# Softmax-free attention, PReLU MLP and soft MoE on one core: reciprocal of the denominator spread by DMA, head pairs of Q three slots apart, K pairs sooner

## The chip, the cores and the metric

The kernel runs on one core of a Trainium2 chip (trn2). The metric is the device time in microseconds of one execution, median of several. TensorE (PE) multiplies, VectorE (DVE) and ScalarE (ACT) work elementwise, GpSimd (POOL) does the reductions over partitions, SyncE (SP) issues every DMA of this kernel, in the order in which they stand in its program.

## The reference

Three stages follow each other on 4608 tokens (8 sequences of 576) of width 512 (8 heads of 64), all in float32, w_in and w_out given as float64.

```python
def phi(x):                                            # w_phi: 64 x 128
    proj = x @ w_phi
    proj = proj - np.max(np.abs(proj), axis=-1, keepdims=True)
    return np.concatenate([np.exp(proj), np.exp(-proj)], axis=-1)
q_p, k_p = phi(q), phi(k)
kv = np.einsum('bhsf,bhsd->bhfd', k_p, v);  z = np.sum(k_p, axis=2)
num = np.einsum('bhsf,bhfd->bhsd', q_p, kv)
den = np.einsum('bhsf,bhf->bhs', q_p, z)[..., None] + 1e-06
x = num / den                                          # attention, 4608 x 512
h = x @ w_in                                           # 512 x 2048
g = np.maximum(h, 0.0) + alpha * np.minimum(h, 0.0)
x = g @ w_out                                          # 2048 x 512
logits = x @ moe2_phi                                  # 32 slots of 8 experts
slot_input = softmax(logits, over tokens).T @ x
slot_out[e] = np.maximum(slot_input[e] @ w1[e], 0.0) @ w2[e]
out = softmax(logits, over slots) @ slot_out
```

## The kernel before, in words

**Blocks and slots.** The tokens are cut into NB = 12 blocks of BT = 384. A block has NC = 16 slots, one for each 128 columns of w_in. In a slot `gemm(n, c)` (L505) issues twelve matmuls of 128x384 in the fp32r format into one PSUM bank `ph`: each of four head pairs k contributes w_hi·x_hi, w_hi·x_lo and w_lo·x_hi, where x is split into `xhi` and `xlo` and w_in likewise. `leaky` (L510 to L520) turns the bank into `gT`, and `turn_g` transposes it on VectorE (L532) and multiplies four of them at a time with `wpr` (w_out times phi, L540). The other matmuls of the kernel (K, Q, V, logits) are in plain fp32, two passes of TensorE for each instruction (the profile counts passes: a group x8 is four instructions).

**K and Q.** `k_pair` (32 of them, two heads of one sequence each) makes the features of K (L289, L280 to L284), the sums K·V (`pkv`, L333 and L339) and turns them (L355) into two tiles, `kv` and `zt`, of which KVB = 6 are kept. `q_pair` (four to a block) projects Q (`pq`, L403), takes the largest absolute value on GpSimd (L415), makes the features `qe` (L425) and calls `attend`: `num` (L435) and `den` (L442). `den` has four column groups of 32 partitions, one for each head of the pair and each half of the features; the sum over the halves isn't made there. A block of 384 may reach into two sequences, and then `segments` cuts both into two pieces.

**The division, `q_finish`.** ScalarE copies `den` and adds 1e-6 (L458); a fp32 matmul with a matrix of zeros and ones (`densum`, L460) adds the halves; VectorE takes the reciprocal of 128x384 (L464); ScalarE and VectorE split it into two fp32r halves `rhl` (L469, L470); eight matmuls with a selecting matrix (`sel`, L477 and L478, two for each head pair) spread it over the 128 partitions of `num`; VectorE multiplies (L484), ScalarE rounds to `xhi` (L485) and VectorE makes `xlo` (L486). `xhi`, `xlo` and `num` have one buffer each, so a head pair of `xhi` is written once the last matmul of the block before has read it.

**Order.** `at(slot, phase, fn)` files each piece of work under a slot and a phase, and the loop at L690 writes the program slot by slot. A list scheduler then orders each engine's instructions by the data they wait for and by their place in that program. Pairs of Q for block n stand at slots 16(n−1)−6, −2, +2 and +6 and `q_finish` at 16(n−1)+11; pair i of K (from i = 8) at slot 6i−42.

**Beside that.** In the first hundred microseconds `conv` (L183 to L214) turns w_in and w_out from float64 words into fp32, mostly on VectorE. wpr needs w_out, so g of blocks 0 and 1 is stored to DRAM (`gT_d`, L521) and read back (`reload`, L522 to L526) in ten extra steps behind slots 84 and 132 (VB = [4, 7]): four tiles at a time into two buffers of 768 KB, `vg0` and `vg1`. From slot 152 on `fetch` fills buffers that have come free with pieces of w_out, w1 and w2 for the soft MoE, in one fixed order; the last of them go into buffers of the tail.

## Time and profile before

| | us |
|---|---|
| median of 3 runs | 1057.03 (1055.14 to 1058.01) |
| profiled execution, its own time | 1057.16 |
| its span, first to last instruction | 1055.4 |
| TensorE busy | 984.1 (93%), mean granted clock 0.964 |
| VectorE busy | 773.8 (73%) |
| ScalarE busy | 469.8 (45%) |
| GpSimd busy | 149.2 (14%) |

Busy time is the time in which at least one instruction of the engine is running. Matmuls are pipelined: each is shown from its start to its modelled end, so the ends of neighbours overlap, and what a group takes on TensorE is the distance from its start to the start of the next group. The timeline gives start and duration of a group of like instructions, and in brackets how long the engine had been idle before it and what ended that.

### The profile page before, as it was taken

To read this page: it belongs to the slowest core of one execution; us is meant where nothing else is said; L and a number is where in the kernel's file an instruction comes from. 1 tells how busy PE (TensorE), PEld (TensorE's weight loads), DVE (VectorE), ACT (ScalarE), POOL (GpSimd) and SP (SyncE) were. 2 spreads that over 40 slices of the span, in tenths; PEclk is the share of its full clock that TensorE was granted. 3 is DMA by queue.
4 is the path that set the end of the run, shared out by engine and by line. 5 is a ranking of instruction groups with operands and counts; after the bars stand their busy time and mean duration, and the time that the engine had idled before them with its cause. 6 is when DMAs were issued, how large, how long until landed. Compare 5 with 4: busy or idle time off the path is not lost.

```text
span 1055.4 us, 21864 instructions
## 1 busy us (share of the span) xinstructions
PE 984.1 (93%) x9038; PEld 685.2 (65%) x9038; DVE 773.8 (73%) x1552; ACT 469.8 (45%) x908; POOL 149.2 (14%) x88
## 2 busy tenths in 40 slices
PE   3787998998999999999999999999999999998994
PEld 1445776774676776676666776767667767787353
DVE  3999989879767578587878687687888486874133
ACT  3876867776444245144235344343334343200133
POOL 2201214121111212121112111121112221000000
PEclk7898999998999999999999999999999999999995
DMA  5343653653010111010401111110401200769879
GB/s 199 120 141 125 193 188 114 225 178 100 9 31 31 39 31 38 20 51 19 163 10 38 32 39 31 31 38 19 160 19 46 96 8 2 249 226 327 261 235 309
DMA packets 71986, 110.60 MB, mean 105 GB/s; under 512 B 7248, under 2 KB 47312, under 8 KB 71888
## 3 DMA queue, kind: packets, MB, share of 16 engines
q1 hardware_dynamic: 71888, 109.22, 32.0%
q8 instruction: 71, 1.16, 0.4%
q14 instruction: 27, 0.22, 0.1%
HBM read 89.27 MB, written 19.92 MB: 103 GB/s over the span
## 4 chain that ended last, share of the span: by engine, by line
PE 71%; DVE 3%; DMA 2%; ACT 1%; issue 1%; DVEq 0%; ACTq 0%; SPq 0%
PE ph L505 34%; PE num L435 5%; PE pS L602 5%; PE pkv L333 5%; PE pl L540 4%; PE den L442 3%; PE pq L403 3%; PE pk L289 2%; DMA out_dram<-os 2%; PE pso L819 1%; PE pe L782 1%; PE sel L477 1%; PE pt L355 1%; PE pr L558 1%; PE densum L460 1%; PE pkv L339 1%
## 5 line engine op out<-in xcount | busy, mean ns | idle before, releaser
L505 PE MATMUL ph<-xhi,w 128*128 128x384 f32 x1536 | 435.2, 351 | 6.5 <-DVE gT L515 4.4
L505 PEld LDWEIGHTS ph<-xhi,w 128*128 128x128 f32 x1536 | 279.0, 189 | 76.8 <-issue 41.5
L505 PE MATMUL ph<-xlo,w 128*128 128x384 f32 x768 | 255.1, 340 | 0.0
L415 POOL PARTITION_ALL_REDUCE mb<-pj x48 | 140.4, 2928 | 553.0 <-ACT pj L409 450.1
L505 PEld LDWEIGHTS ph<-xlo,w 128*128 128x128 f32 x768 | 143.6, 188 | 12.6 <-issue 6.1
L515 DVE SCALAR_TENSOR_TENSOR gT<-gT,alpha_neg,ph 128x384 f32<-128x384 f32 x104 | 62.9, 605 | 77.3 <-ACT ph L514 76.5
L532 DVE STREAM_TRANSPOSE gb<-gT 128x384 f32<-128x384 f32 x192 | 105.6, 566 | 5.7 <-DMA gT<-gT_d 1.9
L513 ACT ACTIVATE gT<-ph 128x384 f32<-128x384 f32 x104 | 50.8, 489 | 114.8 <-PE ph L505 114.0
L425 ACT ACTIVATE qe<-pj 128x768 f32<-128x768 f32 x92 | 73.9, 839 | 59.5 <-DVE pj L419 56.2
L517 DVE TENSOR_SCALAR gT<-ph,alpha_sb 128x384 f32<-128x384 f32 x88 | 53.8, 613 | 46.2 <-PE ph L505 45.8
L333 PE MATMUL pkv<-kp,vt 128*64 128x256 f32 (+1 forms) x640 | 85.0, 400 | 1.1 <-DVE wpr L250 1.1
L435 PE MATMUL num<-qe,kv 128*64 128x192 f32 (+1 forms) x496 | 70.9, 417 | 0.0
L283 ACT ACTIVATE kp<-kp 128x512 f32<-128x512 f32 (+1 forms) x80 | 46.8, 586 | 51.6 <-DVE kp L282 51.1
L333 PEld LDWEIGHTS pkv<-kp,vt 128*64 128x64 f32 (+1 forms) x640 | 41.3, 140 | 39.4 <-issue 17.1
L280 DVE TENSOR_REDUCE mx<-pk 128x4 f32<-128x512 f32 (+1 forms) x80 | 50.2, 627 | 11.4 <-PE pk L289 9.7
L602 PE MATMUL pS<-gb,d 32*32 32x256 f32 x2304 | 55.0, 385 | 0.3 <-DVE logits L594 0.2
L403 PE MATMUL pq<-qraw,wp 64*128 64x384 f32 x192 | 48.9, 562 | 6.7 <-DMA qraw<-in_qT_dram 4.1
L446 ACT COPY num<-num 128x384 f32<-128x384 f32 x48 | 22.8, 475 | 67.1 <-PE num L435 64.2
L409 ACT COPY pj<-pq 128x768 f32<-128x768 f32 x44 | 35.2, 799 | 36.3 <-PE pq L403 36.3
L419 DVE TENSOR_TENSOR pj<-pj,mb 128x768 f32<-128x768 f32 x48 | 46.6, 971 | 6.0 <-POOL mb L415 6.0
L282 DVE TENSOR_TENSOR kp<-pk,mx 128x512 f32<-128x512 f32 (+1 forms) x80 | 50.2, 627 | 0.8 <-PE pkv L333 0.2
L514 ACT ACTIVATE ph<-ph 128x384 f32<-128x384 f32 x104 | 50.6, 487 | 0.0
(191 smaller groups left out, 1345.6 us busy)
## 6 DMA issues: line engine op xcount, KB each, us to landing
w<-in_w_dram SPq DMA_DIRECT2D x58, 256.0 KB, 5.7
qraw<-in_qT_dram SPq DMA_DIRECT2D x48, 192.0 KB, 2.4
out_dram<-os SPq DMA_DIRECT2D x18, 512.0 KB, 3.7
raw<-in_w_in_dram SPq DMA_DIRECT2D x16, 512.0 KB, 3.6
raw<-in_w_out_dram SPq DMA_DIRECT2D x16, 512.0 KB, 4.2
gT_d<-gT SPq DMA_DIRECT2D x32, 192.0 KB, 2.0
gT<-gT_d SPq DMA_DIRECT2D x8, 768.0 KB, 5.2
pf<-in_w_dram SPq DMA_DIRECT2D x21, 256.0 KB, 6.0
```

The lines of the kernel that those rows point to most:

```text
L333: return lambda: nc.tensor.matmul(pkv[64 * j:64 * j + 64, 0:256], vt[:, 64 * j:64 * j + 64], feats(t, j).rearrange("p s f -> p (s f)"), st ...
L403: lambda j=j, sl=slice(64 * j, 64 * j + 64): nc.tensor.matmul(pq[j][:, 0:BT], wp[sl], st["qraw"][sl], start=True, stop=True)
L415: nc.gpsimd.partition_all_reduce(mb, pj, 128, bass_isa.ReduceOp.absmax)
L425: nc.scalar.activation(st["e", s], pj, AF.Exp, scale=(1.0, -1.0)[s])
L435: lambda s=s, j=j: nc.tensor.matmul(num[64 * j:64 * j + 64, o:o + w], kvs[:, s, 64 * j:64 * j + 64], st["e", s][:, j, o:o + w], start=(s = ...
L505: gemm_last[0] = nc.tensor.matmul(h, (w_in_hi, w_in_lo)[a][c][:, 128 * k:128 * k + 128], (xhi, xlo)[b][:, k, :], start=(i == 0), stop=(i = ...
L513: nc.scalar.activation(gT, h, AF.Relu, scale=-1.0)
L514: nc.scalar.activation(h, h, AF.Relu)
L515: nc.vector.scalar_tensor_tensor(out=gT, in0=gT, scalar=alpha_neg[:, c:c + 1], in1=h, op0=ALU.mult, op1=ALU.add)
L517: nc.vector.tensor_scalar(out=gT, in0=h, scalar1=0.0, scalar2=alpha_sb[:, c:c + 1], op0=ALU.min, op1=ALU.mult)
L532: nc.vector.transpose(out=gb[n, c // 8][:, c % 8, :], in_=gT)
L602: lambda j=j, i=i, h=h: nc.tensor.matmul(pS[i][32 * (j % 4):32 * (j % 4) + 32, 256 * h:256 * h + 256], st["d"][32 * i:32 * i + 32, 32 * j: ...
```

## The change

- **Denominator.** `den` is now written by eight matmuls of 192 columns for each head pair, whatever the sequences: the tile holds the four column groups (head, half of the block) at 192 columns each, and the sum over feature halves and head pairs is left in PSUM. VectorE adds 1e-6 and takes the reciprocal of 128x192; two DMAs write it to DRAM (`rc_d`), and two more read it back with a step of zero over 64 partitions into `bc`, 128x1536. VectorE multiplies `num` by `bc`, all from SBUF. The matrices `densum` and `densel` with their setup, the matmuls `densum` and `sel`, and the split `rhl` are gone.
- **Places.** Pairs of Q stand three slots apart and `q_finish` at 16(n−1)+7, the read-back `widen` a slot later, division and `scale` six slots later; the division is held behind the last `leaky` or `conv` instruction of the slots up to there (`mark`). KVB is 8, and K pairs come up to eight slots sooner.
- **Read-back of g.** Two tiles at a time in three buffers `vg`, and four of the sixteen tiles through the ring of `gT`, which has five buffers.
- **Fetches.** `bc` and `vg` give three pieces each where `rhl`, `densel`, `vg0` and `vg1` gave eight; the pool `pf` opens at slot 168 in place of 170.

```diff
-KVB = 6
+KVB = 8
...
+    rc_d = [dram.tile([2, 32, 2, HB], F32, name=f"rc_d{i}") for i in range(2)]
...
-            for b, o, w in segments(n):
-                kvs, zt = kv_t[NP * b + p]
+            for s in (1, 0):
                 together([
-                    lambda g=g: nc.tensor.matmul(
-                        den[32 * g:32 * g + 32, o:o + w], zt[:, g, :], st["e", g % 2][:, g // 2, o:o + w],
-                        start=(p == 0 and o == 0), stop=(p == NP - 1 and o + w == BT))
-                    for g in (3, 1, 2, 0)])
+                    lambda j=j, h=h, zt=kv_t[NP * ((n * BT + h * HB) // S) + p][1]: nc.tensor.matmul(
+                        den[64 * j + 32 * h:64 * j + 32 * h + 32, 0:HB], zt[:, 2 * j + s, :],
+                        st["e", s][:, j, HB * h:HB * h + HB],
+                        start=(p == 0 and s == 1), stop=(p == NP - 1 and s == 0))
+                    for j in (1, 0) for h in (1, 0)])
...
         def recip():
-            rc = st["rc"] = sm.tile([128, BT], F32, tag="dT", name="rc")
-            nc.vector.reciprocal(out=rc, in_=st["ps"][:, 0:BT])
...
+            rd = sm.tile([128, BT], F32, tag="dT", name="rd")[:, 0:HB]
+            nc.vector.tensor_scalar(out=rd, in0=st["den"][:, 0:HB], scalar1=1e-6, scalar2=None, op0=ALU.add)
+            nc.vector.reciprocal(out=rd, in_=rd)
+            for j in range(2):
+                nc.sync.dma_start(rc_d[n % 2][j].rearrange("p h t -> h p t"), rd[64 * j:64 * j + 64])
+
+        def widen():
+            bc = st["bc"] = xp.tile([128, NP, BT], F32, tag="bc", name="bc")
+            for j in range(2):
+                nc.sync.dma_start(
+                    bc[64 * j:64 * j + 64], rc_d[n % 2][j, 0:NP].rearrange("p h t -> p (h t)").unsqueeze(0).to_broadcast([64, NP, BT]))
...
-                nc.vector.tensor_tensor(out=xs, in0=st["sel", p][:, 0:BT], in1=xs, op=ALU.mult)
...
+                ins = nc.vector.tensor_tensor(out=xs, in0=st["bc"][:, p, :], in1=xs, op=ALU.mult).ins
+                tc.add_manual_dep(ins, mark[max(k for k in mark if k <= slot + 6)].name, nosync, reason="behind the load")
...
     def reload(n, c):
-        gT4 = attk.tile([128, 4, BT], F32, tag=f"vg{c // 4 % 2}", name="gT4")
-        nc.sync.dma_start(gT4, gT_d[n, c:c + 4].rearrange("c p t -> p c t"))
-        for j in range(4):
-            gT_t[n, c + j] = gT4[:, j]
+        if c in (6, 8):
+            for j in range(2):
+                gT_t[n, c + j] = sm.tile([128, 512], F32, tag="gT", name="gT2", bufs=5)[:, 0:BT]
+                nc.sync.dma_start(gT_t[n, c + j], gT_d[n, c + j])
+            return
+        gT2 = attk.tile([128, 2, BT], F32, tag="vg", name="gT2", bufs=3)
+        nc.sync.dma_start(gT2, gT_d[n, c:c + 2].rearrange("c p t -> p c t"))
...
-        k_pair(int(-40 + 2.5 * i) if i < 4 else int(-20 + 6 * (i - 4)) if i < 8 else 6 * i + -42, i)
+        k_pair(int(-40 + 2.5 * i) if i < 4 else int(-20 + 6 * (i - 4)) if i < 8 else 6 * i - 42 - min(i - 8, 8), i)
...
-                q_pair(NC * (n - 1) + 4 * p + -6 + (-1 if n == 1 else 0), n, p)
-        q_finish(-39 + 18 + 5 if n == 0 else NC * (n - 1) + -6 + 12 + 5 + (-1 if n == 1 else 0), n)
+                q_pair(NC * (n - 1) + 3 * p - 6 - (p > 0 or n == 1), n, p)
+        q_finish(-39 + 18 + 5 if n == 0 else NC * (n - 1) + 7, n)
```

What this does to the order of three engines:

TensorE at the border between blocks 5 and 6, before (`w_1268` is the last piece of w_in, `w_637` and `w_690` are the two halves of the first; `pk` belongs to a pair of K):

```order
L289 MATMUL pk<-wp,kraw 128x128 x8
L505 MATMUL ph<-xhi,w_1268 128x384
L477 MATMUL sel<-rhl,densel 128x384 x2
L478 MATMUL sel<-rhl,densel 128x384 x2
L477 MATMUL sel<-rhl,densel 128x384
L478 MATMUL sel<-rhl,densel 128x384
L442 MATMUL den<-qe,zt 32x192 x8
L477 MATMUL sel<-rhl,densel 128x384
L478 MATMUL sel<-rhl,densel 128x384
L505 MATMUL ph<-xhi,w_637 128x384 x4
```

The same border in the changed kernel (`w_1256` last piece, `w_630` and `w_659` first):

```order
L491 MATMUL ph<-xlo,w_1256 128x384
L491 MATMUL ph<-xhi,w_1256 128x384
L278 MATMUL pk<-wp,kraw 128x128 x8
L491 MATMUL ph<-xhi,w_630 128x384 x6
L532 MATMUL pl<-gT,wpr 32x384 x4
L491 MATMUL ph<-xhi,w_659 128x384
```

The eight `sel` matmuls are gone, the `den` of the next block's first pair stands elsewhere, and only one group stands between the last product of a block and the first of the next.

VectorE while the division of block 1 is made, before (`mx`, `kp`, `kv`, `zt` belong to pairs of K, `pj` to a pair of Q, `gT` to `leaky`):

```order
L464 RECIPROCAL rc<-densum 128x384
L515 SCALAR_TENSOR_TENSOR gT<-gT,alpha_neg,ph 128x384
L470 TENSOR_TENSOR rhl<-rc,rhl 128x384
L362 COPY kv<-pt 128x256
L363 COPY zt<-pt 128x4
L515 SCALAR_TENSOR_TENSOR gT<-gT,alpha_neg,ph 128x384
L280 TENSOR_REDUCE mx<-pk 128x4
L282 TENSOR_TENSOR kp<-pk,mx 128x4x128
L484 TENSOR_TENSOR num<-sel,num 128x384
L280 TENSOR_REDUCE mx<-pk 128x4
L419 TENSOR_TENSOR pj<-pj,mb 128x768
L484 TENSOR_TENSOR num<-sel,num 128x384
```

The same place in the changed kernel (`w_1675` is a piece of w_out in conversion):

```order
L447 TENSOR_SCALAR rd<-den 128x192
L448 RECIPROCAL rd<-rd 128x192
L315 TENSOR_TENSOR ks<-ks,kp 64x512
L501 SCALAR_TENSOR_TENSOR gT<-gT,alpha_neg,ph 128x384
L471 TENSOR_TENSOR num<-bc,num 128x384 x4
L269 TENSOR_REDUCE mx<-pk 128x4
L351 COPY kv<-pt 128x256
L352 COPY zt<-pt 128x4
L198 TENSOR_TENSOR w_1675<-m,sign 128x512
L465 TENSOR_TENSOR xlo<-num,xhi 128x384 x2
L408 TENSOR_TENSOR pj<-pj,mb 128x768
L465 TENSOR_TENSOR xlo<-num,xhi 128x384
```

Two instructions stand between the reciprocal and the four multiplications, which now stand in a row.

SyncE's queue at the same place, before:

```order
L520 DMA gT_d<-gT 128x384 x3
L269 DMA kraw<-in_kT_dram 128x512
L520 DMA gT_d<-gT 128x384
L391 DMA qraw<-in_qT_dram 128x384
L520 DMA gT_d<-gT 128x384 x2
L269 DMA kraw<-in_kT_dram 128x640
L391 DMA qraw<-in_qT_dram 128x384
```

And in the changed kernel:

```order
L507 DMA gT_d<-gT 128x384 x3
L258 DMA kraw<-in_kT_dram 128x512
L507 DMA gT_d<-gT 128x384
L450 DMA rc_d_75<-rd 2x32x192 x2
L455 DMA bc<-rc_d_75 64x1536
L380 DMA qraw<-in_qT_dram 128x384
L455 DMA bc<-rc_d_75 64x1536
L507 DMA gT_d<-gT 128x384
```

Four DMAs have come in, and the load of Q stands between the two reads of the reciprocal.

## Rows read from the trace of the kernel before

**Rows 1.** The page: its first line and busy time by engine.

```profile
span 1055.4 us, 21864 instructions
PE 984.1 (93%) x9038; PEld 685.2 (65%) x9038; DVE 773.8 (73%) x1552; ACT 469.8 (45%) x908; POOL 149.2 (14%) x88
```

**Rows 2.** Busy by stretch: sum, PE, PEld, DVE, ACT, POOL, clock, DMA share, GB/s.

```profile
60.00:100.00 40.00, 32.72 (x319) 20.34 (x317) 39.86 (x79) 29.90 (x58) 0.00 (x0) 0.87 0.35 112
100.00:140.00 40.00, 37.98 (x327) 28.89 (x325) 38.65 (x68) 32.04 (x63) 11.25 (x6) 0.96 0.64 207
...
400.00:500.00 100.00, 100.00 (x811) 67.08 (x808) 74.99 (x151) 41.85 (x82) 17.24 (x9) 1.00 0.11 33
...
970.00:1020.00 50.00, 47.92 (x465) 22.80 (x466) 8.88 (x53) 10.51 (x25) 1.90 (x2) 0.93 0.87 278
```

**Rows 3.** Timeline of PE: densum, two sel matmuls, and what follows.

```profile
459.66 0.91 PE L460 MATMUL densum<-rd,densum 128*128 128x384 f32 x2
460.50 2.53 PE L333 MATMUL pkv<-kp,vt 128*64 128x256 f32 x20
...
474.06 0.33 PE L477 MATMUL sel<-rhl,densel 128*128 128x384 f32 x1
474.23 0.33 PE L478 MATMUL sel<-rhl,densel 128*128 128x384 f32 x1
```

**Rows 4.** Timeline of PE: den in one piece, halved, in two segments.

```profile
454.94 0.85 PE L442 MATMUL den<-qe,zt 128*32 128x384 f32 x8
455.72 0.92 PE L403 MATMUL pq<-qraw,wp 64*128 64x384 f32 x4
...
481.15 0.84 PE L442 MATMUL den<-qe,zt 128*32 128x384 f32 x4
481.92 0.62 PE L505 MATMUL ph<-xlo,w 128*128 128x384 f32 x2
...
147.52 0.86 PE L442 MATMUL den<-qe,zt 128*32 128x192 f32 x16
148.31 0.49 PE L305 MATMUL pk<-wp,kraw 64*128 64x128 f32 x4
```

**Rows 5.** Timeline of PE: from fp32 into fp32r and out again.

```profile
442.33 0.44 PE L505 MATMUL ph<-xhi,w 128*128 128x384 f32 x1
442.61 0.34 PE L505 MATMUL ph<-xlo,w 128*128 128x384 f32 x1
...
453.23 0.34 PE L505 MATMUL ph<-xhi,w 128*128 128x384 f32 x1
453.50 1.51 PE L435 MATMUL num<-qe,kv 128*64 128x384 f32 x8
```

**Rows 6.** Timeline of PE beside the first read-back of g.

```profile
552.38 0.69 PE L477 MATMUL sel<-rhl,densel 128*128 128x384 f32 x1 [1.84 <-DVE num L484]
```

**Rows 7.** Instructions by line, VectorE: busy us, mean ns, idle before.

```profile
L464 DVE RECIPROCAL rc<-densum 128x384 f32<-128x384 f32 x12 | 30.7, 2557 | 21.7 <-PE densum L460 21.7
...
L470 DVE TENSOR_TENSOR rhl<-rc,rhl 128x384 fp32r<-128x384 f32 x12 | 7.6, 632 | 0.0
...
L165 DVE CAST densel<-ident 128x64 fp32r<-128x64 f32 x8 | 1.5, 186 | 0.0
L162 DVE TENSOR_TENSOR densum<-ident 128x16 f32<-128x16 f32 x8 | 1.3, 166 | 0.0
```

**Rows 8.** DMA issues: count, KB each, median us from issue to landing.

```profile
raw<-in_w_in_dram SPq DMA_DIRECT2D x16, 512.0 KB, 3.6
...
gT<-gT_d SPq DMA_DIRECT2D x8, 768.0 KB, 5.2
...
wo<-w SPq DMA_DIRECT2D x64, 64.0 KB, 1.7
```

**Rows 9.** Timeline of SP's queue near the end: the last four loads of weights.

```profile
1010.31 2.58 SPq L686 DMA_DIRECT2D w<-in_w_dram  x4
```

**Rows 10.** Timeline of PE near the end: the products that use those weights.

```profile
1020.43 2.36 PE L819 MATMUL pso<-w,hTm 128*32 128x256 f32 x38
```

More of the change, by code (lines that the diff above doesn't have):

```diff
@@ L131, in attention_prelu_softmoe @@
     ones = const.tile([128, 32], F32, name="ones")
-    eps_den = const.tile([128, 1], F32, name="eps_den")
-    densum = att.tile([128, 128], F32, name="densum")
-    densel = xp.tile([128, NP, 128], F32R, tag="densel", name="densel")
     wpr = sm.tile([128, NC, NSL], F32, tag="wpr", name="wpr")
@@ L157, in setup_b @@
             nc.vector.tensor_tensor(out=o, in0=o, in1=ident[:, 96:128], op=ALU.add)
-        for p in range(NP):
-            for j in range(2):
-                a, b = 64 * j + p, 64 * j + 32 + p
-                r = 32 * p + 16 * j
-                nc.vector.tensor_tensor(
-                    out=densum[:, r:r + 16], in0=ident[:, a:a + 1].to_broadcast([128, 16]),
-                    in1=ident[:, b:b + 1].to_broadcast([128, 16]), op=ALU.add)
-                nc.vector.tensor_copy(densel[:, p, 64 * j:64 * j + 64], ident[:, r:r + 1].to_broadcast([128, 64]))
     sched = {}
+    mark = {}
     after = [NC * (b + 1) + VR for b in VB]
@@ L208, in second @@
             w = prep.tile([128, 512], F32, tag="w32", name="w32", bufs=2)
-            nc.vector.tensor_tensor(out=w, in0=m, in1=st["sign"], op=ALU.mult)
+            mark[slot + 1] = nc.vector.tensor_tensor(out=w, in0=m, in1=st["sign"], op=ALU.mult).ins
             use(slot, w)
@@ L487, in scale, with divide, go @@
             return go
-        at(slot, "pe", sums)
+        def divide(p):
+            def go():
+                xs = st["num"][:, p, :]
+                ins = nc.vector.tensor_tensor(out=xs, in0=st["bc"][:, p, :], in1=xs, op=ALU.mult).ins
+                tc.add_manual_dep(ins, mark[max(k for k in mark if k <= slot + 6)].name, nosync, reason="behind the load")
+            return go
         at(slot, "post", recip)
-        at(slot + 1, "pre", split)
+        at(slot + 1, "pre", widen)
         for p in range(NP):
-            at(slot + 1, "post", spread(p))
-            at(slot + 1, "post", scale(p))
+            at(slot + 6, "post", divide(p))
+        for p in range(NP):
+            at(slot + 6, "post", scale(p))
     gb, pl_t, gT_t = {}, {}, {}
@@ L715, in attention_prelu_softmoe @@
                 fetch(attk, tag)
-            for tag in ("vg0", "vg1"):
-                fetch(attk, tag, 3)
+            for i in range(3):
+                fetch(attk, "vg", 1, 3)
             for i in range(KPB):
                 fetch(attk, "kp2", 2, KPB)
-        if slot == 170:
+        if slot == 168:
             close_pool("attq")
@@ L726, in attention_prelu_softmoe @@
             fetch(xp, "num", 3)
-            fetch(xp, "rhl")
-            fetch(xp, "densel")
+            fetch(xp, "bc", 3)
         if NC * (NB - 1) < slot <= nslots:
```

45 lines of the change are left out of this document (17 added, 28 removed).

## The prediction

> **What bounds the kernel now.** I read the page first. TensorE is busy for 984.1 of 1055.4 us and VectorE for 773.8 [rows 1], so a shorter program on TensorE pays as long as TensorE is what the stage waits for. Whether it is, the stretches tell. From 400 to 500 us TensorE is busy for 100.00 of 100 us at full clock while VectorE has 25 us free [rows 2]; the stretches up to 930 us look alike. There every matmul removed is time removed, unless something new makes TensorE wait. From 60 to 140 us it is the other way round: VectorE is busy for 39.86 and 38.65 of 40 us, and TensorE idles for 7.3 of the first 40 [rows 2]. That is the conversion of w_in and w_out, and there only less VectorE work pays. From 970 us on the load of weights matters too: the DMA engines are busy for 0.87 at 278 GB/s [rows 2].
>
> The price of a matmul I read from starts, not from durations, since durations overlap: from the start of a group to the start of the next.
>
> **What goes from TensorE.**
> 1. *sel.* A matmul of 128x384 in fp32r takes 474.23 − 474.06 = 0.17 us in a run [rows 3]. There are 96 of them: −16.3 us.
> 2. *densum.* From 459.66 to 460.50 is 0.84 us [rows 3], times 12: −10.1 us.
> 3. *den.* Before, a group of four matmuls of 384 columns takes 0.78 us; a group that is split in two, with half of the matmuls, takes 0.77 us for each half; and a group over two sequences, eight matmuls of 192 columns, takes 0.79 us [rows 4]. So what counts is the round in which four column groups run side by side, and half a round costs as much as a whole one. Counted in the order before: 25 whole groups, 12 halves and 4 single ones make 41 rounds, 41 × 0.78 = 32.0 us, and 16 groups over two sequences 16 × 0.79 = 12.6 us; together 44.6. After: 99 rounds of four matmuls of 192 columns at 0.79 / 2 = 0.395, 39.1 us. That gives −5.5 us.
> 4. *Changes of format.* Going from fp32 into fp32r makes the first product take 442.61 − 442.33 = 0.28 in place of 0.17 us, and the last product ahead of an fp32 group takes 453.50 − 453.23 = 0.27 [rows 5]; one excursion costs 0.21 us. The order has 219 excursions before and 201 after: −3.8 us.
> 5. One group of num stands in two pieces in the changed order, which by the same law of halves costs half of 454.94 − 453.50 [rows 4, 5]: +0.7 us.
>
> The sum is −35.0 us. Blocks are alike, so a twelfth, 2.9 us, belongs to block 0, which lies in the stretch where VectorE sets the time, and doesn't count: **−32.1 us**.
>
> **The start.** For block 0 VectorE saves half of a reciprocal of 2.557 us (half the columns), a subtraction of 0.632 us, and the setup of densum and densel, 1.5 + 1.3 us [rows 7]; it gains the addition of 1e-6 on 192 columns, at most a subtraction's 0.63 us. That is −4.1 us. Counted over the whole order with the trace's duration for each form, the work ahead of the first g falls from 77.8 to 70.6 us, since some of it also moves behind. I take **−5 us**, nearer to the first, because what is moved behind comes back in a stretch where VectorE is full as well; bounds 0 and −7.
>
> **Read-back of g.** In the ten extra steps there is no fp32r product to fill TensorE, and before the change it waits for the multiplication of sel by VectorE, 1.84 us [rows 6], and in the same way at the second of the two places. This chain is gone: **−3.7 us**. What is late next is the read-back itself. Before, one DMA of 768 KB lands after 5.2 us [rows 8]. Now four tiles go through the ring of gT, of which leaky then has one buffer left, and on SyncE's queue the four DMAs of the reciprocal stand ahead of the remaining tiles. In each place the tiles behind them come at the earliest after a write (1.7 us, the 64 KB row of rows 8) and the queue's issues; TensorE and VectorE have other work of about that length. I take **+2 us** for the two together, bounds 0 and +10 (twice 5.2, a whole load laid bare).
>
> **The new chain of the division.** From the last den: addition and reciprocal, 0.63 + 2.557 / 2 = 1.9 us at most [rows 7]; write of 48 KB, 1.7 us [rows 8]; two reads of 393 KB, at most 3.6 us by the row of 512 KB [rows 8], and up to two issues ahead of the second, 0.65 us each by the slowest row there is (four in 2.58 us) [rows 9]; multiplication and rounding, two passes of some 0.63 us [rows 7]. Sum 9.8 us. VectorE is in order: behind a division that waits stand the K features, and behind these the leaky that frees a PSUM bank for gemm. SyncE is in order too: the reads wait for the write to land, and loads of Q, K and V stand behind them. In blocks 2 to 11 the order has 4 to 10 leaky instructions between reciprocal and division, that is 4 slots of 12 × 0.17 us on TensorE at least, plus the fp32 groups beside them, so the chain is hidden; block 0 lies in the stretch that VectorE fills. Block 1 is the weak place: one leaky lies between, and TensorE has, from the last den of block 1 to its first gemm, twelve fp32r products (2.0 us), ten K·V matmuls (2.5 us, the row at 460.50 [rows 3]), a projection of Q (0.9 us [rows 4]) and five short groups of about half a microsecond (by the row of 0.49 us [rows 4]), about 8 us. 9.8 − 8 is 1.8: **+2 us**, bounds 0 and +6 (the chain with every DMA twice as slow).
>
> One rule of the Trainium skill bears on this chain. No row of before shows a transfer whose slowest dimension is 2; the nearest, 64 KB from 32 partitions, lands after 1.7 us [rows 8]. "DMA: Bandwidth & Descriptors", section "Why a DMA increments its semaphore by 16 and not by 1", says that a DMA uses the largest number of engines up to 16 that divides the slowest dimension of both sides; the write of the reciprocal has 2 there and would run on two engines. By it and 278 GB/s over all 16 [rows 2] each of the two engines would need about 1.4 us for 24 KB, an estimate, and with a fixed part of its own the write would come up to 1 us later, the forecast with it. The sum above goes without it.
>
> **The tail.** Two pieces more (46 in place of 44) go into buffers that are used a second time. By 278 GB/s [rows 2] two pieces of 256 KB are 1.9 us. The last four are issued from 1010.31 to 1012.9 [rows 9], and their products run from 1020.43 to 1022.8 [rows 10]; the last piece lands 4.0 us ahead of its use. The delay is hidden: 0, bounds 0 and +1.5. If that slack were gone it would cost the 1.9.
>
> **Edits at nothing.** Opening pf two slots sooner and eight K buffers add no work. K pairs up to eight slots sooner put at most one and a half pairs more of VectorE work into blocks 0 and 1; between 140 and 260 us there is little room, and I keep +6 us as a bound, and −4 for TensorE's waits for VectorE there that could close.
>
> **The sum.** 1055.4 − 32.1 − 5 − 3.7 + 2 + 2 = 1018.6 us span. The profiled execution took 1057.16 with a span of 1055.4, so 1.8 lie outside; it is within 0.13 us of the median 1057.03. **1018.6 + 1.8 = 1020 us.**
>
> **Rivals.**
> - *The early stretch eats part of it.* VectorE is full up to 140 us and nearly full after it; the divisions of blocks 0 and 1 no longer wait for TensorE but for DMAs, and K work comes sooner. For it: rows 2, and the short cover of block 1. Against it: VectorE's total falls. Then the start brings −1, block 1 costs 6 and the read-back 6: 1055.4 − 32.1 − 1 − 3.7 + 6 + 6 + 1.8 = 1032 us.
> - *Waits close too.* The start brings 7, the waits up to 260 us close by 4, the read-back and block 1 cost nothing, and block 0's matmuls count: 1055.4 − 35.0 − 7 − 3.7 − 4 + 1.8 = 1007.5 us. For it: TensorE's idle time up to 260 us is mostly put down to VectorE. Against it: VectorE has little left to give there.
> - *The reciprocal is late at every block (slower).* SyncE's queue is in order, and a load of V or Q that waits for TensorE to free its buffer may stand ahead of a read of the reciprocal. Then VectorE stops at the division, leaky stops, and gemm has no bank. A slot of gemm with what stands beside it is about 5 us (a block takes 78 us); if 11 blocks lose one, +55: 1075 us. It decides from 37 / 11 = 3.4 us a block on. Against it: four slots or more lie between reciprocal and division in ten blocks.
> - *The change doesn't do what it says.* If removed matmuls were filled by waits of the same length, for instance since leaky or the K features are what the slot waits for, the time stays at 1057. Against it: 100.00 of 100 us on TensorE with VectorE at 75 [rows 2].
>
> **How the numbers follow.** Forecast 1020 (1012 to 1026): 0.60. Early stretch, 1032: 0.18. Waits close, 1007.5: 0.13. Late at every block, 1075: 0.05. Nothing, 1057: 0.04. The range reaches over the first three, 1007 to 1034, and leaves out the last two and some edges. A difference below 0.3% (3 us) can't be told from no change with this kernel. Faster takes the first three cases and what of the last lies below: 0.92; same 0.03; slower 0.05.
>
> **What would show it.** Right: TensorE's busy time falls by about 35 us; stretches in the middle stay at 100 of 100; no wait at a division on VectorE from block 2 on. The new chain: VectorE's wait for bc at block 1 of some 2 us. Start: the first g comes about 5 us sooner. Wrong: waits for DMA named at the division in several blocks, gemm waiting for leaky behind it, or a group of four den matmuls of 192 columns that takes more than 0.4 us.

## The result: 1032 us against 1058, faster, and 12 us short of the forecast

| | before | changed kernel |
|---|---|---|
| median | 1057.52 us (1055.14 to 1061.49) | 1032.19 us (1030.36 to 1035.08) |
| span of the profiled execution | 1055.4 us | 1028.5 us |
| ratio | | 0.9759, interval 0.9722 to 0.9797 |

The forecast was 1020 (1007 to 1034). The time lies in the range, at the figure of the first rival (1032). The profiled execution of the changed kernel is the fastest of its four (1030.36 us), so spans differ by 26.9 us and medians by 25.3. The page of the changed kernel, first line and busy time by engine, against [rows 1]:

```profile
span 1028.5 us, 22249 instructions
## 1 busy us (share of the span) xinstructions
PE 949.9 (92%) x9174; PEld 671.7 (65%) x9174; DVE 762.9 (74%) x1533; ACT 452.5 (44%) x884; POOL 146.4 (14%) x88
```

TensorE's busy time fell from 984.1 to 949.9, that is by 34.2 us, and the forecast was 35.0. But the span fell by 26.9 only: the time in which TensorE runs nothing grew from 1055.4 − 984.1 = 71.3 to 1028.5 − 949.9 = 78.6 us. The forecast had it fall by 1.8 (36.8 for the span less 35.0). So the question is where 7.3 us of new waiting came from.

The stretches of the changed kernel (sum, PE, PEld, DVE, ACT, POOL, granted clock, DMA share, GB/s), against [rows 2]:

```profile
60.00:100.00 40.00, 33.43 (x345) 21.07 (x343) 36.66 (x77) 28.17 (x55) 0.00 (x0) 0.91 0.48 137
100.00:140.00 40.00, 36.89 (x326) 28.51 (x323) 39.59 (x68) 31.52 (x62) 9.68 (x5) 1.00 0.64 208
140.00:180.00 40.00, 34.27 (x284) 24.77 (x285) 29.98 (x61) 25.99 (x53) 6.41 (x5) 0.91 0.45 130
...
400.00:500.00 100.00, 99.83 (x1025) 67.42 (x1026) 78.61 (x156) 42.48 (x80) 17.31 (x9) 1.00 0.19 52
```

and the third of them before the change:

```profile
140.00:180.00 40.00, 38.75 (x303) 28.84 (x304) 34.61 (x59) 26.60 (x53) 13.11 (x7) 1.00 0.39 124
```

The middle is as full as it was (99.83 of 100). New is the stretch from 140 to 180 us: TensorE, VectorE and ScalarE are all less busy than before, and the clock is granted at 0.91 in place of 1.00. So all three wait for something else there. The timeline of VectorE at the divisions of blocks 0 and 1 (start, duration, in brackets the idle time before and what ended it) says for what:

```profile
85.80 1.96 DVE L471 TENSOR_TENSOR num<-bc,num 128x384 f32<-128x384 f32 x4 [3.31 <-DMA bc<-rc_d]
...
165.32 1.97 DVE L471 TENSOR_TENSOR num<-bc,num 128x384 f32<-128x384 f32 x4 [5.37 <-DMA bc<-rc_d]
```

and TensorE at the first product of block 1:

```profile
166.48 1.97 PE L491 MATMUL ph<-xhi,w 128*128 128x384 f32 x5 [5.72 <-ACT xhi L464]
```

The reciprocal's way through DRAM is late at blocks 0 and 1. At blocks 2 to 11 VectorE never waits at a division.

A second comparison serves all experiments below: when the first product of a block starts on TensorE. It tells where a gain or loss arises, which two total times don't.

| first product of block | before | changed | difference |
|---|---|---|---|
| 0 | 88.9 | 89.6 | +0.7 |
| 1 | 164.9 | 166.5 | +1.5 |
| 4 | 400.3 | 394.9 | −5.4 |
| 8 | 704.5 | 687.3 | −17.2 |
| last product ends | 954.5 | 925.7 | −28.8 |
| end of the span | 1055.4 | 1028.5 | −26.9 |

One caution goes with it. The list scheduler orders each kernel anew, so an edit at one block also moves work elsewhere. Of the variants of the changed kernel below, only the one without the trips of blocks 2 to 11 has the changed kernel's order on TensorE and VectorE; the others differ from it from the first product of block 1 on at the latest. So a difference of one or two us between two first products may be one of order.

### The profile page after: what moved, and what is told of

Same layout as the page of the kernel before. It is cut to its first block, busy times and chain, and to the rows that moved or that the text cites. A ratio compares the mean times of both kernels' runs of the same rounds, so it can differ in the third digit from the quotient of the medians.

```text
span 1028.5 us, 22249 instructions
## 1 busy us (share of the span) xinstructions
PE 949.9 (92%) x9174; PEld 671.7 (65%) x9174; DVE 762.9 (74%) x1533; ACT 452.5 (44%) x884; POOL 146.4 (14%) x88
## 4 chain that ended last, share of the span: by engine, by line
PE 63%; DVE 19%; ACT 7%; DMA 5%; issue 4%; POOL 0%; SPq 0%; DVEq 0%; ACTq 0%; POOLq 0%
PE ph L491 31%; PE num L424 5%; PE pkv L322 5%; PE pS L594 4%; PE pl L532 3%; PE den L430 3%; PE pq L392 3%; DMA out_dram<-os 2%; DVE gb L524 2%; DVE mx L269 2%; PE pso L813 2%; PE pk L278 1%; PE pe L776 1%; DVE m L196 1%; DVE gT L501 1%
## 5 line engine op out<-in xcount | busy, mean ns | idle before, releaser
L491 PEld LDWEIGHTS ph<-xhi,w 128*128 128x128 f32 x1536 | 278.8, 188 | 81.6 <-issue 39.3
L404 POOL PARTITION_ALL_REDUCE mb<-pj x48 | 138.0, 2876 | 542.2 <-ACT pj L398 453.5
L424 PE MATMUL num<-qe,kv 128*64 128x192 f32 (+1 forms) x496 | 71.3, 413 | 2.7 <-ACT qe L414 2.1
L278 PE MATMUL pk<-wp,kraw 64*128 64x128 f32 x512 | 39.0, 294 | 16.2 <-issue 11.6
L424 PEld LDWEIGHTS num<-qe,kv 128*64 128x64 f32 x496 | 31.9, 136 | 28.3 <-issue 18.1
```

The source lines that it names most:

```text
L404: nc.gpsimd.partition_all_reduce(mb, pj, 128, bass_isa.ReduceOp.absmax)
L424: lambda s=s, j=j: nc.tensor.matmul(num[64 * j:64 * j + 64, o:o + w], kvs[:, s, 64 * j:64 * j + 64], st["e", s][:, j, o:o + w], start=(s = ...
L491: gemm_last[0] = nc.tensor.matmul(h, (w_in_hi, w_in_lo)[a][c][:, 128 * k:128 * k + 128], (xhi, xlo)[b][:, k, :], start=(i == 0), stop=(i = ...
```

## Experiments

### 1. What the round trip costs in all

Edit: the four DMAs of each block are gone; `bc` is one tile, filled once.

```diff
-            for j in range(2):
-                nc.sync.dma_start(rc_d[n % 2][j].rearrange("p h t -> h p t"), rd[64 * j:64 * j + 64])
...
-            bc = st["bc"] = xp.tile([128, NP, BT], F32, tag="bc", name="bc")
-            for j in range(2):
...
+            st["bc"] = bc_all
```

> Changed kernel without the four DMAs per block that write the reciprocal to DRAM and read it back spread: num is multiplied by a constant tile filled once (so the division by the denominator is left out, the reciprocal itself is still computed). Theory (the round trip through DRAM is what the early VectorE-bound stretch waits for): VectorE's waits of 3.3 us at the division of block 0 and 5.4 us at that of block 1 and TensorE's 5.7 us ahead of the first product of block 1 vanish, the first product of block 2 comes 6 to 9 us sooner than 245.5 us, the time is 1023 to 1026 us against 1032. Rival (the K pairs that come sooner fill the early stretch): the waits vanish but the first product of block 2 moves by less than 2 us, time 1030 to 1032. Rival (the 10.6 MB more that the DMA engines move hold up all other loads): besides the early waits those at the read-back of g and in the tail fall too, time below 1021.

Measured: 1019.7 us (1019.56 to 1021.17), 12.5 us less than the changed kernel. The first product of block 0 comes at 81.6, of block 1 at 152.7, of block 4 at 384.2 in place of 394.9: 10.7 of the gain are there by block 4, and 1.2 more come from there to the end of the last product (913.8 against 925.7), of which the tail gives 1.2 back. The first product of block 2 comes at 228.5, that is 17.0 us sooner, where the theory gave 6 to 9; what exceeds 10.7 is gone again by block 3. The time without the trip is the forecast figure, 1020, in part by luck: without the trip the start gains 7.3 us in place of the 5 forecast, and the tail is 3.2 us longer than before the change in place of 0. The total lies below the band that the theory gave and inside that of the rival on traffic. That rival holds for a small part: between the first products of blocks 5 and 10 TensorE's idle time falls from 8.9 to 6.1 us and the time by 1.3, but the tail doesn't get shorter. The rival with the K pairs falls.

### 2. Which blocks pay

Three kernels leave out the round trip of block 0, of block 1, and of blocks 2 to 11. For block 0 (the others test `n == 1` and `n >= 2`):

```diff
             nc.vector.reciprocal(out=rd, in_=rd)
+            if n == 0:
+                return
...
+            if n == 0:
+                st["bc"] = bc_all
+                return
```

> Changed kernel without the round trip of block 0 alone: its num is multiplied by a constant tile, so the division of block 0 is left out; blocks 1 to 11 as changed. Without any round trip the kernel took 1019.7 us against 1032. Theory (the round trips of blocks 0 and 1 cost it about half each, since each ends in a wait of its own): the first product of block 0 comes about 6 to 8 us sooner than 89.6, that of block 4 some 4 to 7 us sooner than 394.9, time 1025 to 1028. Rival (VectorE is full behind block 0, so what block 0 gains is given back by block 1): the first product of block 0 is sooner, that of block 1 and of block 4 within 2 us of before, time 1030 to 1033.

> Changed kernel without the round trip of block 1 alone (its division left out, multiplied by a constant). Theory (half of the loss each): TensorE's wait of 5.7 us ahead of the first product of block 1 is gone, that of block 4 comes 4 to 7 us sooner than 394.9, time 1025 to 1028. Rival (block 1 is the whole loss): first product of block 4 at 384 to 386, time 1019 to 1022.

> Changed kernel without the round trips of blocks 2 to 11 (their division left out, multiplied by a constant tile that is filled once); blocks 0 and 1 as changed. Theory (from block 2 on the trip is hidden behind four slots or more): within 2 us of the changed kernel, 1030 to 1033. Rival (the queue of SyncE and the traffic cost something at every block): 1025 us or less.

| trip left out | time, us | against 1032.2 | first product of block 0, 1, 4 |
|---|---|---|---|
| block 0 | 1032.2 (1031.3 to 1034.5) | 0 | 80.7, 164.6, 394.3 |
| block 1 | 1024.4 (1019.6 to 1025.4) | −7.8 | 91.1, 160.0, 389.0 |
| blocks 2 to 11 | 1029.1 (1025.3 to 1029.6) | −3.1 | 88.9, 166.1, 394.6 |
| all | 1019.7 | −12.5 | 81.6, 152.7, 384.2 |

For block 0 the rival is right: its first product comes 9.0 us sooner, but that of block 1 only 1.9 and that of block 4 0.6. TensorE and VectorE of that kernel at block 1:

```profile
164.56 2.61 PE L499 MATMUL ph<-xhi,w 128*128 128x384 f32 x7 [6.54 <-ACT xhi L472]
```

```profile
163.40 1.96 DVE L479 TENSOR_TENSOR num<-bc,num 128x384 f32<-128x384 f32 x4 [5.52 <-DMA bc<-rc_d]
```

Both wait longer than in the changed kernel (5.72 and 5.37): what block 1 starts on, its reciprocal's trip, is hardly sooner, so a sooner block 0 ends in a longer wait. Its gain can be kept only when block 1 doesn't wait. So the parts don't add up: at block 4 all trips together give 10.7 us, the three parts 0.6, 5.9 and 0.3. (In the times all together give 1.6 us more than the parts, which is within their spread.)

Block 1 alone costs 7.8 us, more than its wait of 5.7. The rest shows in the clock. The stretch from 140 to 180 us of the kernel without block 1's trip, and in the changed kernel the stretch from the end of the wait to 170.7 us:

```profile
140.00:180.00 40.00, 39.98 (x324) 30.92 (x324) 37.19 (x69) 29.80 (x60) 9.10 (x6) 1.00 0.47 151
```

```profile
166.48:170.70 4.22, 4.22 (x20) 3.40 (x21) 4.22 (x10) 2.52 (x7) 0.00 (x0) 0.50 0.14 35
```

The first is at full clock. In the second the granted clock is 0.50, the lower of the two levels of 2.4 and 1.2 GHz, for 4.22 us of work, of which half is lost: about 2.1 us, an estimate. With the wait that is 7.8. The five products behind the wait take 1.97 us, where a run takes 0.17 each [rows 3].

Leaving out the trips of blocks 2 to 11 brings about 3 us. The theory's band began at 1030, so it is missed by 1 us, but the ratio to the kernel before, 0.9716 (0.9695 to 0.9738), overlaps that of the changed kernel (0.9722 to 0.9797), so the 3 us aren't clear of the spread. No wait at a division is behind them. In the profiled execution 2.0 us have come by the end of the last product, and 1.3 of these are given back behind it. Part of the 2.0 is a wait at the second read-back of g: TensorE waits there for the tiles for 0.23 us, in the changed kernel for 1.13 (its row stands below, at the read-back):

```profile
727.44 0.85 PE L541 MATMUL pl<-gT,wpr 128*32 128x384 f32 x8 [0.23 <-DMA gT<-gT_d]
```

The order of work is the same in both, so this wait comes from the trips' DMAs. What the rest is stays open.

### 3. Is it VectorE's idle time that costs, or the late start of block 1?

Edit: the divisions of blocks 0 and 1 are held behind further conversion work.

```diff
+                if n in late:
+                    tc.add_manual_dep(ins, cmark[max(k for k in cmark if k <= slot + late[n])].name, nosync, reason="behind the conversion")
...
+        late = {0: 13, 1: 8}
```

> Changed kernel with the divisions of blocks 0 and 1 held behind one conversion step more of w_in and two more of w_out, so that VectorE has 2.5 and about 5 us of other work in its queue while the reciprocal is under way; nothing else changed. Theory (idle VectorE time during the round trip is lost because VectorE sets the pace up to 260 us): VectorE's waits at the two divisions fall from 3.3 and 5.4 us to under 1.5 each, TensorE's wait ahead of block 1 stays or grows by some us, the first product of block 2 comes 4 to 8 us sooner than 245.5, time 1024 to 1028. Rival (TensorE waits for xhi in any case, and what counts is when block 1 starts): the first product of block 1 is later and block 2 no sooner, time 1031 to 1036.

Measured: 1031.7 us (1029.6 to 1034.2), no difference. VectorE's waits did shrink, to 0.87 and 0.94 us:

```profile
84.40 1.96 DVE L473 TENSOR_TENSOR num<-bc,num 128x384 f32<-128x384 f32 x4 [0.87 <-DMA bc<-rc_d]
...
161.90 1.96 DVE L473 TENSOR_TENSOR num<-bc,num 128x384 f32<-128x384 f32 x4 [0.94 <-DMA bc<-rc_d]
163.78 0.68 DVE L273 TENSOR_TENSOR kp<-pk,mx 128x512 f32<-128x512 f32 x1
```

and the wait of TensorE took another name:

```profile
164.52 1.65 PE L394 MATMUL pq<-qraw,wp 64*128 64x384 f32 x4 [4.03 <-DVE kp L273]
166.10 1.33 PE L497 MATMUL ph<-xhi,w 128*128 128x384 f32 x3
```

The projection of Q waits for the K features (`kp`), which stand behind the division in VectorE's queue. The first product of block 1 stays at 166.1, that of block 2 at 245.7 and that of block 4 at 395.3. So my theory that idle VectorE time is the loss fell. The rival had the time and block 2 right, but block 1 is no later; that the start of block 1 counts is shown by experiment 2, not by this one.

### 4. Is the write slow because it runs on few DMA engines?

Edit: each write of two groups of 32 rows is cut into two DMAs of 32 rows.

```diff
-                nc.sync.dma_start(rc_d[n % 2][j].rearrange("p h t -> h p t"), rd[64 * j:64 * j + 64])
+                for h in range(2):
+                    nc.sync.dma_start(rc_d[n % 2][j, :, h], rd[64 * j + 32 * h:64 * j + 32 * h + 32])
```

> Changed kernel with each write of the reciprocal cut into two of 32 rows (slowest dimension 32 in place of 2, the same bytes). If the writes are slow because a slowest dimension of 2 puts them on two DMA engines (the Trainium skill, DMA: Bandwidth & Descriptors, Why a DMA increments its semaphore by 16 and not by 1), the read is issued 1 us or more sooner after the first write than the 2.9 us of block 1, its wait falls from 5.4 to about 4.5 us, time 1030 to 1032. If a fixed cost of a write through DRAM sets it, the two more issues of about 0.6 us make the read as late or later: 2.9 to 4.2 us, wait 5.4 to 6.5, time 1032 to 1034.

SyncE's queue at block 1 in the changed kernel, and in this one:

```profile
155.72 1.13 SPq L450 DMA_DIRECT2D rc_d<-rd  x2
158.66 0.50 SPq L455 DMA_DIRECT2D bc<-rc_d  x1
159.26 0.53 SPq L380 DMA_DIRECT2D qraw<-in_qT_dram  x1
159.88 0.48 SPq L455 DMA_DIRECT2D bc<-rc_d  x1
```

```profile
153.65 1.71 SPq L451 DMA_DIRECT2D rc_d<-rd  x4
155.61 0.45 SPq L456 DMA_DIRECT2D bc<-rc_d  x1
156.16 0.53 SPq L380 DMA_DIRECT2D qraw<-in_qT_dram  x1
156.79 0.45 SPq L456 DMA_DIRECT2D bc<-rc_d  x1
```

From the first write to the first read, which waits for the write to land, it is 158.66 − 155.72 = 2.94 us before and 155.61 − 153.65 = 1.96 us with the cut, although two more DMAs are issued. VectorE's wait at the division falls from 5.37 to 4.09, TensorE's from 5.72 to 3.38. That is about the 1 us that the prediction had estimated for two engines and kept out of its sum. The stretch of the changed kernel in which its two writes are all that moves (DMA share next to last) shows the engines:

```profile
157.00:159.00 2.00, 2.00 (x21) 1.31 (x19) 0.00 (x0) 0.57 (x2) 2.00 (x1) 1.00 0.13 38
```

A share of 0.13 of 16 engines is two engines. By the rule of the Trainium skill ("DMA: Bandwidth & Descriptors", "Why a DMA increments its semaphore by 16 and not by 1"), the largest number up to 16 that divides the slowest dimension of both sides, it is two for the write as it was; the trace agrees.

The first product of block 4 comes 1.1 us sooner, that of block 9, behind the second read-back of g, 1.2 later, and the total is 1032.4 us (1031.0 to 1034.6): a gain of that size can't be told from none.

### 5. What the rest of the change costs: K pairs and read-back

The division, `den` and the places of the Q pairs as before, all the rest of the change kept. Against the kernel before, in short:

```diff
-KVB = 6
+KVB = 8
...
-        gT4 = attk.tile([128, 4, BT], F32, tag=f"vg{c // 4 % 2}", name="gT4")
+        gT2 = attk.tile([128, 2, BT], F32, tag="vg", name="gT2", bufs=3)
...
-        k_pair(int(-40 + 2.5 * i) if i < 4 else int(-20 + 6 * (i - 4)) if i < 8 else 6 * i + -42, i)
+        k_pair(int(-40 + 2.5 * i) if i < 4 else int(-20 + 6 * (i - 4)) if i < 8 else 6 * i - 42 - min(i - 8, 8), i)
```

> Kernel before (densum and sel matmuls, head pairs of Q four slots apart) with the rest of the change: eight K buffers, K pairs up to eight slots sooner, read-back of g in pairs and through the ring of gT, the pieces of vg. Theory (the gain is that of the matmuls removed, the rest costs nothing or a few us): 1057 to 1062 us, TensorE busy 983 to 986. Rival (the rest of the change costs much, and the matmul part alone would have brought all of the forecast 37 us): 1066 us or more. Rival (the rest brings part of the gain): 1050 us or less.

Of that, the read-back of g alone (the second of the three edits; KVB and the K pairs as before):

> Kernel before with the changed read-back of g alone (two tiles at a time in three buffers, four tiles through the ring of gT, three pieces of vg in the fetch); six K buffers, K pairs and the division as before. The rest of the change without the division took 1067 us against 1058. Theory (the read-back costs about 4 us of that, the K pairs the other): TensorE's waits in blocks 5 to 9 grow by 2 to 3 us at each of the two places, time 1061 to 1064, and nothing moves before 500 us. Rival (all of it is the K pairs): 1057 to 1060. Rival (all of it is the read-back): 1066 or more.

The changed kernel with the K pairs at their slots of before:

```diff
-        k_pair(int(-40 + 2.5 * i) if i < 4 else int(-20 + 6 * (i - 4)) if i < 8 else 6 * i - 42 - min(i - 8, 8), i)
+        k_pair(int(-40 + 2.5 * i) if i < 4 else int(-20 + 6 * (i - 4)) if i < 8 else 6 * i - 42, i)
```

> Changed kernel with the K pairs at the slots of before (6i-42, nothing sooner); eight K buffers and all else as changed. Theory (K work brought forward into the full early stretch costs part of the 8.5 us that the rest of the change costs): the first product of block 2 and of block 4 come 3 to 8 us sooner than 245.5 and 394.9 us, of which what is only moved comes back by block 10; time 1026 to 1030. Rival (head pairs three slots apart need the K tiles sooner, so the later K pairs make TensorE wait at num and den): waits for kv or zt appear from block 2 on, time 1033 to 1040. Rival (the read-back of g is the whole loss): within 2 us of 1032.

| | time, us | ratio to before, interval |
|---|---|---|
| old division, the rest changed | 1067.3 (1065.8 to 1069.5) | 1.0084, 1.0065 to 1.0104 |
| before, new read-back alone | 1060.1 (1057.8 to 1062.3) | 1.0014, 1.0001 to 1.0027 |
| changed, K pairs as before | 1044.1 (1041.1 to 1045.2) | 0.9861, 0.9834 to 0.9888 |

The read-back costs 1.5 us, as the rival with the K pairs had it and less than I expected, although TensorE's waits between the first products of blocks 5 and 10 grow from 4.3 to 9.5 us, as much as my theory had: a wait is not its price in time. With the old division and Q pairs four slots apart, the sooner K pairs (with two more buffers) cost the other 7 us. The first product of block 4 already comes 10.3 us later with them (408.3 against 398.0); why is open. With the new division and Q pairs three slots apart they gain 12. Read the other way, with the rest of the change alike, the new division, `den` and places of the Q pairs bring 1067.3 − 1032.2 = 35.1 us. My rival for the later K pairs had that sign (1033 to 1040), but not the size, and I had looked for the waits at num and den. The timeline of VectorE at blocks 7 and 10, with the K pairs as before, shows one reason:

```profile
611.48 1.96 DVE L471 TENSOR_TENSOR num<-bc,num 128x384 f32<-128x384 f32 x4 [3.36 <-DMA bc<-rc_d]
...
836.55 1.96 DVE L471 TENSOR_TENSOR num<-bc,num 128x384 f32<-128x384 f32 x4 [6.39 <-DMA bc<-rc_d]
```

and TensorE at the first product of block 10:

```profile
839.18 1.90 PE L491 MATMUL ph<-xhi,w 128*128 128x384 f32 x8 [2.60 <-ACT xhi L464]
```

In that kernel the last den matmul of block 10 starts only 15 us ahead of the first product of the block (824.0 and 839.2); in the changed kernel it is 28 (805.2 and 833.2). K pairs that come later make the last den later, and then the trip through DRAM is no longer hidden: my rival of a late reciprocal, in two blocks, for want of K. These waits of TensorE are part of the 12 us only. The last product ends 13.7 us later than in the changed kernel (939.4 and 925.7), and 7.7 of these come between the first products of blocks 10 and 11, behind the late division: the granted clock there is 0.94 in place of 1.00, which is 3.4 us of 56.6, and TensorE runs 495 matmul passes in place of 470, since `num` and `den` of the next block's pairs, which need the K tiles, lie later. What makes up the rest is open.

### 6. Matmuls again for the early blocks

Edit: blocks 0 and 1 (or 1 alone) split the reciprocal into fp32r halves and spread it by matmuls with a selecting matrix; the others go through DRAM. Their division is filed five slots sooner with it, and is not held behind `leaky` or `conv`. For blocks 0 and 1, in short (for block 1 alone the test is `n == 1`):

```diff
+                for h in range(2):
+                    for r in ("rhi", "rlo"):
+                        nc.tensor.matmul(ps[:, HB * h:HB * h + HB], densel[:, p, h, :], st[r], start=(r == "rhi"), stop=(r == "rlo"))
...
-        at(slot + 1, "pre", widen)
+        at(slot + 1, "pre", split if n < NDEF else widen)
```

> Changed kernel in which blocks 0 and 1 spread their reciprocal by matmuls with a selecting matrix again (in fp32r halves, sixteen matmuls of 192 columns a block, from the new den of 192 columns) and only blocks 2 to 11 go through DRAM. Without any round trip the kernel took 1019.7 us. Theory (the round trip costs its 12 us at blocks 0 and 1 alone): TensorE's wait of 5.7 us ahead of block 1 is gone, the matmuls and the split cost 2 to 4 us in the early stretch, time 1021 to 1026. Rival (the DMAs of the other ten blocks cost as much, through queues and traffic): 1029 to 1033.

> As e_hyb, and with the K pairs at the slots of before. If the two losses are separate they add up: the time is that of e_hyb less what e_kbefore gains over the changed kernel's 1032, 1017 to 1024. If both free the same wait in the early stretch, it equals the better of the two alone, 1021 to 1028.

> Changed kernel in which block 1 alone spreads its reciprocal by matmuls with a selecting matrix (sixteen fp32r matmuls of 192 columns, from the new den); block 0 and blocks 2 to 11 go through DRAM. Leaving out the round trip of block 1 brought 7.8 us (1024.4). Theory (block 1's chain through DRAM is the loss, and a chain through PSUM in its place costs only its matmuls and the split, 2 to 4 us): TensorE's wait of 5.7 us ahead of the first product of block 1 falls under 1, the first product of block 4 comes 3 to 6 us sooner than 394.9, time 1026 to 1029. Rival (the matmuls, the split and the setup of the matrix cost the full early stretch as much as the trip does, as in the kernel where blocks 0 and 1 both went back): 1031 to 1033.

| matmuls in blocks | time, us | first product of block 1, 4, 8 | last product ends |
|---|---|---|---|
| none (changed kernel) | 1032.2 (1030.4 to 1035.1) | 166.5, 394.9, 687.3 | 925.7 |
| 0 and 1 | 1032.6 (1026.7 to 1034.1) | 156.8, 391.2, 683.7 | 924.9 |
| 0 and 1, K pairs as before | 1041.4 (1040.4 to 1046.5) | 156.4, 387.4, 684.5 | 935.7 |
| 1 alone | 1031.4 (1028.3 to 1034.6) | 158.0, 390.2, 683.1 | 921.8 |

The wait ahead of block 1 is gone and the clock is full. Timeline of TensorE with the matmuls in block 1 alone, and its stretch from 140 to 180 us:

```profile
154.41 1.33 PE L472 MATMUL sel<-rhl,densel 128*128 128x192 f32 x8 [0.57 <-ACT rhl L464]
155.91 1.16 PE L284 MATMUL pk<-wp,kraw 64*128 64x128 f32 x16 [0.17 <-ACT pj L404]
157.00 1.14 PE L472 MATMUL sel<-rhl,densel 128*128 128x192 f32 x8
157.98 1.05 PE L516 MATMUL ph<-xhi,w 128*128 128x384 f32 x5
```

```profile
140.00:180.00 40.00, 39.26 (x329) 29.14 (x328) 35.32 (x63) 28.65 (x56) 11.43 (x7) 1.00 0.38 118
```

The first product of block 1 comes 8.5 us sooner, that of block 4 4.7 and that of block 8 4.2. The profiled execution keeps 3.9 to the end of the last product and 2.0 to the end of its span; the medians differ by 0.8 us, within their spread, so I can't call this kernel faster than the changed one. With both blocks on matmuls the same happens: 3.7 us at block 8, and 0.8 at the last product. I expected 3 to 6 us in the time. The kernel with both blocks on matmuls lies in the band of the rival on the other ten blocks, but experiment 2 gave these about 3 us, not 12. Where the gain goes behind block 8 is seen in part: from the first product of block 8 to that of block 10 the kernel with block 1 on matmuls takes 147.9 us against 145.9, beside the second read-back of g, and its tail takes 1.9 us more. The sooner start isn't what lengthens the first of the two: the kernel of experiment 3, whose block 8 starts 1.7 us later than that of the changed kernel, takes 148.3. Two things differ there. The clock falls in the kernel with block 1 on matmuls:

```profile
720.00:725.00 5.00, 4.35 (x28) 1.79 (x30) 4.01 (x7) 0.87 (x2) 0.00 (x0) 0.66 0.91 217
```

A mean of 0.66 is 3.4 of 5 us at the lower level, which costs up to 1.7 us; in the changed kernel the clock is full at this place (1.00 from 724 to 734 us), behind waits that are no shorter. And the order is another one, in the changed kernel:

```profile
761.88 1.16 PE L278 MATMUL pk<-wp,kraw 64*128 64x128 f32 x16 [0.64 <-DVE acc L606]
762.98 1.32 PE L491 MATMUL ph<-xhi,w 128*128 128x384 f32 x6
```

and with block 1 on matmuls:

```profile
762.05 2.53 PE L328 MATMUL pkv<-kp,vt 128*64 128x256 f32 x20
764.51 1.68 PE L516 MATMUL ph<-xhi,w 128*128 128x384 f32 x8
```

How much each of the two costs no run separates. With the K pairs as before it is 1041.4, outside both bands that I gave for it, so there is no second gain to add. So leaving out the trip of block 1 shows what it costs, but no kernel here that still divides block 1 by its denominator has won these 7.8 us back.

## Why the prediction was right and where it was not

| step | forecast, us | what the runs show |
|---|---|---|
| TensorE's work | −35.0, of it −32.1 counted | busy −34.2 |
| start | −5 | first product of block 0 +0.7; without trips −7.3 (81.6) |
| division of block 1 | +2 | +7.8 (left out alone) |
| divisions of blocks 2 to 11 | 0 | +3.1 (left out alone), within the spread |
| read-back of g | −3.7 + 2 | TensorE's waits beside it +4.6 |
| tail | 0 | +2.0 |
| sooner K pairs | 0 | −12 with the new division, about +7 with the old |

**TensorE's work was right.** The page shows 34.2 us. That it agrees to 1 us is in part luck, since the busy time of one page depends on the clock of that execution: the kernel of experiment 4, with as many matmul passes (9174) and the same time, has 958.9 us in place of 949.9, and before the change the new read-back alone has 980.2 in place of 984.1. The unit of den holds too: eight matmuls of 192 columns, two rounds, take 0.79 us in the changed kernel, as [rows 4] have it for two segments:

```profile
427.17 0.86 PE L430 MATMUL den<-qe,zt 128*32 128x192 f32 x16
427.96 0.44 PE L491 MATMUL ph<-xhi,w 128*128 128x384 f32 x1
```

**The step that failed is the chain of the division**, "Sum 9.8 us" against a cover of about 8. The cover was right: the last den of block 1 ends at 152.3, and TensorE's other work ends at 160.8. The chain was mis-sized. The reciprocal ends at 155.69, since VectorE had 1.6 us of other work ahead of it; from there to the division it is 165.32 − 155.69 = 9.6 us, of which I had put 6.6 (1.7 for the write, 1.3 for issues, 3.6 for the read). The write took 2.9 us to the first read, whereas I took the 64 KB row (1.7) and kept the sentence on two engines out of the sum; the second read was issued 1.2 us later, and 5.4 us passed from there to the division. For the read I had taken the row of 512 KB (3.6), as if two DMAs of 393 KB each that are under way together landed as one. In the changed kernel's trace no landing of theirs is recorded; in that of experiment 4 the two at block 1 land 5.1 us after their issue (median):

```profile
bc<-rc_d SPq DMA_DIRECT2D x2, 384.0 KB, 5.1
```

Meanwhile the DMA engines of the changed kernel are busy for 0.85 of the time from 160.77 to 166.48 us, with the load of Q between the two reads; what the reads would take without it no run shows. Then the wait was counted at its length alone, not with the clock that falls behind it, about 2.1 us more. The bound of +6 for block 1 was too small for the 7.8.

**Block 0** was not asked at all: "block 0 lies in the stretch that VectorE fills". The stretch was full because VectorE had work in its queue; with a division ahead of that work, which waits for a DMA, the queue stands (3.31 us), full or not. So the 5 us of the start didn't come. That the loss is not additive I didn't see either: as long as block 1 waits, block 0 costs nothing (experiment 2).

**The read-back** lost the two waits of 1.84 us [rows 6], as said. But the new waits were larger than the +2. Between the first products of blocks 5 and 10 TensorE idles for 8.9 us in the changed kernel and for 4.3 before. The second of the two places:

```profile
724.89 1.50 PE L532 MATMUL pl<-gT,wpr 128*32 128x384 f32 x16 [1.90 <-DVE acc L606]
...
729.82 0.85 PE L532 MATMUL pl<-gT,wpr 128*32 128x384 f32 x8 [1.13 <-DMA gT<-gT_d]
731.39 0.44 PE L491 MATMUL ph<-xhi,w 128*128 128x384 f32 x1 [0.72 <-DVE gT L501]
```

It waits for VectorE first and for the tiles only then. That the DMAs of the reciprocal hold up these tiles, as the prediction had it, is seen in experiment 2: without the trips of blocks 2 to 11 the wait of 1.13 us is 0.23. But these waits are not all lost time: the old kernel with the new read-back alone has as many of them and was 1.5 us slower; that part I had about right.

**The tail** is 2.0 us longer, and no wait of TensorE for a load of weights is seen in it. TensorE stands near its start without a releaser that the profile names, 2.82 us here and 1.83 before:

```profile
940.47 1.16 PE L107 MATMUL spin<-ident 128*128 128x128 f32 x9 [2.82 <-issue]
```

```profile
969.91 0.41 PE L757 MATMUL pg<-tident,acc 128*128 128x32 f32 x2 [1.83 <-issue]
```

That is 1.0 of the 2.0 us. TensorE is also busy for 1.1 us longer in the tail, 82.0 us at a mean clock of 0.85 against 81.0 at 0.86. In the three kernels with the old division this stall was 1.1 to 1.8 us, in the eleven others 1.9 to 3.4. The cause of the stall stays open.

**"Edits at nothing"** was wrong of the K pairs. I looked for their VectorE work, a price, and not for the deadline that they serve. The sooner K pairs are what gives the trip its cover in blocks 7 and 10 (experiment 5).

The first rival gave 1032 with +6 for block 1 and a start of −1, and both are within 2 us of what the runs show. That its sum meets the time is in part luck: for the read-back it had −3.7 + 6 where TensorE's waits grew by 4.6 and are not all lost time, and it had nothing for the tail. It had a chance of 0.18. The rival of a reciprocal late at every block did not come; with the K pairs at their slots of before it came in two blocks.

## What to carry to other kernels

A detour through DRAM that takes work off the busiest engine pays where enough other work stands between its ends (here the trip alone took 9.6 us); count that cover for each block, the first ones above all, and look which other edits of the change make it. An engine that is full is no cover for a wait in its own queue: an instruction that waits for a DMA stops the work behind it. A wait of TensorE can cost more than its length, by the slower clock behind it, or less, where the work is only moved. And where a scheduler orders the program anew for each edit, compare the orders before a small difference is put down to the edit.

## What the runs showed of the hardware that I had not expected

- Two DMA writes of 48 KB whose slowest dimension is 2 kept 0.13 of the 16 DMA engines busy and held the read behind them for 2.94 us; each cut into two of 32 rows, with two more issues, they held it for 1.96 us (experiment 4).
- After waits of 4.0 to 6.5 us ahead of block 1 the first products ran at the lower clock (granted at 0.50 from 166.48 to 170.70 us in the changed kernel): three took 1.33 us, five 1.97 and seven 2.61, where five without the wait took 1.05 (experiments 2, 3 and 6).
